# Decode attention over a cache: the last head's keys and softmax ahead of the preceding head's products with v

## The chip, the cores and the metric

The kernel runs on one core of one Trainium2 chip. The metric is device time in microseconds for one execution. The engines named below are PE (matrix products, with its own row PEld for weight loads), DVE and ACT (element-wise work, reductions, exponentials), POOL (one power per norm) and SP, which issues nearly all loads. All float data is 32 bits wide.

## The reference

Two layers, each an attention block and an MLP block, for one new token of width 640, with the same weights and the same cache in both layers:

```
x = x + attention(layernorm(x), k_cache, v_cache, wq, wo)
x = x + mlp(layernorm(x), w1, w2)
x = x + attention(layernorm(x), k_cache, v_cache, wq, wo)
x = x + mlp(layernorm(x), w1, w2)

attention(x): q = (x @ wq) in 32 heads of 128
              p = softmax(q . k * 128**-0.5) over 8192 cached positions
              o = p . v ;  return o (32*128 wide) @ wo
mlp(x):       return max(x @ w1, 0) @ w2          # hidden width 1728
```

The keys of one head are 8192 x 128 floats, 4 MB, and its values are another 4 MB; 32 heads make 268 MB, read once per layer apart from what is kept on the chip.

## The kernel before

**Head by head.** A head's keys come transposed, in four runs of four blocks. `scores` multiplies them by the head's query, which `spread` puts into one column of a 32-column operand, so that 16 rows of one 128 x 512 tile hold all 8192 scores (L366). `exponentials` takes the maximum of each row (L378) and the exponentials with their row sums (L385). `turn` brings the exponentials into columns (L393, L401). `rows_weighed` makes the weights by which the 16 rows, each with its own maximum, are put together (L406 to L416); it is a generator, and its steps are set between other work. `values` multiplies the turned exponentials by v (L427), and `output` copies the sums (L444, L445), multiplies them by the row weights on PE (L453) and leaves the head's 128 outputs in a column of `o_cols` (L460). For the last head of a layer `output` copies in two parts (L447, L449), so that the first copy does not wait for the last piece of v.

**The ring.** Keys and values go into one buffer, `ring`, of 3496 columns of eight floats: three halves of a head (1024 columns each) and 424 more. `todo` is the list of all loads in order. `pump` takes the next load from its head as soon as `place` finds a free stretch, and issues it on SP's queue (L133). It is called from `release`, that is, each time a piece has been used for the last time. One load waits behind another: SP issues them in order. Most heads are two loads of 4 MB, keys and values; the heads near the layers' ends are cut into smaller ones (`UNITS`). The last head of a layer has its keys in two loads of 2 MB and its values in four (2 MB, 1 MB, 768 KB, 256 KB); the head before it has, of its values, two of 2 MB.

**The turn between the layers.** Layer 0 goes through heads 0 to 31, layer 1 through heads 31 to 0. When layer 0 ends, the ring holds all of head 31 and the last of head 30's keys and its values. These stay and are used again by layer 1, so no load into the ring can begin until layer 1 has gone through a piece of head 31. The first four loads of head 30's keys go, for layer 1, into four weight buffers that have become free (`load_beside`, L147).

**The order on the engines.** The schedule is written out by hand: each engine does its instructions in the order of the program text. Work that is not a head's own (projections of earlier heads' outputs by `wo`, queries of the next four heads, products of weights that shorten the layer's end) stands in two lists, `chores` and `slow`; `side_work` does one PE step and one DVE step of them, and is called between the pieces of keys and of values. `due(h)` puts entries on the lists when head `h` begins. Two chores belong to the layer's end. `first_of_last` projects the first two heads of the last group of four. `before_last` projects the third (L332), adds the residual (L642), centres the row (`centred`, L245 to L259), in layer 0 begins layer 1's first query (L655), and makes five steps of `hidden` (L582): the MLP's first product for everything but the last head's share, which `mlp` adds when the last head's outputs are there. After the last head `mlp` finishes the layer; in layer 0 it also makes the query of head 31 for layer 1.

**Buffers that order work.** `p` is one buffer: a head's exponentials and the copy that `output` makes of a head's sums (`oc`) share it. `pT`, the turned exponentials, is one buffer, too. `h_t` holds a head's small columns. The score tiles `ps` are two banks.

**At the end of a layer**, before the change, the order on PE is: scores of the next-to-last head (30 in layer 0, 1 in layer 1), its `turn` and weights, its products with v, its `output`; then the last head's scores, with the steps of `before_last` between their pieces; its `turn` and weights; its products, with the rest of `before_last` after the second piece; its `output`; `mlp`.

Of the kernel before, what the change touches and what calls it, by code (L numbers as in the profile page):

```python
# [10 lines left out]
F32 = mybir.dt.float32  # L11
# [4 lines left out]
P = 128  # L16
D = 640
H = 32
# [5 lines left out]
HG = 4  # L24
# [16 lines left out]
UNITS = {h: WHOLE for h in range(H)}  # L41
# [38 lines left out]
def decode_kernel(ctx: ExitStack, tc: tile.TileContext, x, kv, wq, wo, w1, w2, out):  # L80
# [3 lines left out]
    work = ctx.enter_context(tc.tile_pool(name="work", bufs=1))  # L84
# [268 lines left out]
    def spread_column(q):  # L353
        nc.vector.tensor_copy(
# [3 lines left out]
    def spread(h):  # L358
        spread_column(qT[h // HG][:, h % HG : h % HG + 1])
# [79 lines left out]
    def output(hd, col):  # L439

        oc = work.tile([P, 5, DH], F32, name="p")
        pt = ps_m.tile([P, 512], F32, name="pm")
        if hd.out is hd.out_3:
            nc.vector.tensor_copy(oc[:, :2], hd.out[:, :2])  # L444
            nc.scalar.copy(oc[:, 2:4], hd.out[:, 2:])  # L445
        else:
            nc.vector.tensor_copy(oc[:, :3], hd.out[:, :3])  # L447
            yield
            nc.vector.tensor_copy(oc[:, 3], hd.out_3[:, 3])  # L449
            in_wait(384)  # L450
        n = 1 if hd.out is hd.out_3 else 64
        for r in range(4):
            nc.tensor.matmul(  # L453
                pt[:, :n],
                oc[:, r],
                hd.w[:, r : r + 1].to_broadcast([P, n]),
                start=(r == 0),
                stop=(r == 3),
            )
        nc.vector.tensor_copy(col, pt[:, :1])  # L460
# [130 lines left out]
    def attention_and_mlp(L, xr, s, before=None):  # L591
# [77 lines left out]
        def due(h):  # L669

            where = heads.index(h)
            k, j = divmod(where, HG)
            if j == 0:
                o_cols[k] = work.tile([P, HG], F32, name="o_cols", bufs=2)
            if where and j == 0:
                chores.append([run_out(k - 1), "pe"])
            if j == 2 and k + 1 < NG:
                slow.append([queries_of(k + 1), "pe"])
            if where == H - 2:
                chores.append([first_of_last(), "pe"])  # L680
            if where == H - 1:
                chores.append([before_last(), "pe"])
            if L == 0 and where == 4:
                nc.scalar.dma_start(w1_t, w1)
            if L == 0 and where == 7:
                nc.scalar.dma_start(w2_t, w2)
            if L == 0 and where == 9:
                n = NB * DH * (HG - 1)
                nc.scalar.dma_start(wqc.rearrange("p c d -> p (c d)"), wq[P * (NG - 1) :, n:])
            if L == 0 and where == MIX_AT[0][-1]:  # L690
                slow.append([centred_weights(), "pe"])
            if where == WC_AT[L]:
                nc.scalar.dma_start(mix[:, :D], wo[last // HG][:, last % HG])
            if where == WC_AT[L] + 1:
                slow.append([mixing(), "dve"])
            if where in MIX_AT[L]:
                slow.append([mixing_quarter(MIX_AT[L].index(where)), "pe"])
            if L == 0 and where == MIX_AT[L][-1] + 1:
                slow.append([leading_of_output(), "pe"])
            if where in LEAD_AT[L]:  # L700
                slow.append([leading(LEAD_AT[L].index(where)), "pe"])

        def side_work():
            work_off("pe")
            work_off("dve")
# [3 lines left out]
        def begun(where):  # L709

            nonlocal r
            h = heads[where]
            due(h)
            hd = Head(h)
            pieces = list(pieces_of(L, h, "k"))
            for a, (piece, at) in enumerate(pieces):
                scores(hd, piece, at, a == 0, a == len(pieces) - 1)
                if L and where == 0:
                    r = next(before)
                elif a < len(pieces) - 1:  # L720
                    side_work()
                if h == last and a == 1:
                    side_work()
            return hd

        hd = None
        for where, h in enumerate(heads):
            hd = hd or begun(where)
            if L and where == 0:
                exponentials(hd, r[0])  # L730
                xr, xc = next(before)
                load_wq(groups[1], nc.scalar)
            else:
                exponentials(hd)
            side_work()
            if h == last:
                side_work()
# [5 lines left out]
            hd.out = outs[count[0] % 2]  # L743
            count[0] += 1
            hd.out_3 = outs[count[0] % 2] if h == last else hd.out
            if h == last:
                o = work.tile([P, 1], F32, name="c_ol")
                rest = output(hd, o)
            pieces = list(pieces_of(L, h, "v"))
            for a, (piece, at) in enumerate(pieces):  # L750
                values(hd, piece, at, a == 0, a == len(pieces) - 1)
                if a == 0:
                    at_once(weighing)
                    if h != last:
                        spread(heads[where + 1])
                if a < len(pieces) - 1 and (h != last or a == 1):
                    side_work()
                if h == last and a == len(pieces) - 2:
                    next(rest)
            if h == last:  # L760
                at_once(rest)
            else:
                k, j = divmod(where, HG)

                ahead = begun(where + 1) if L and where < 2 else None
                at_once(output(hd, o_cols[k][:, j : j + 1]))
                hd = ahead
        assert not chores and not slow

        return mlp(L, o, last, *mlp_in)  # L770
# [236 lines left out]
```

## Time and profile before

| | us |
|---|---|
| runs of before (median of 3) | 1367.77 |
| runs of before, lowest and highest | 1365.71, 1371.56 |
| profiled execution, span from first to last instruction | 1368.2 |
| PE busy, whole span | 1006.9 |
| DVE busy, ACT busy | 182.4, 113.3 |

The profiled execution has no time of its own beside its span; the span lies within the runs. Mean granted clock of PE is 0.807. A line of the timeline gives the start in us from the first instruction, the busy time, the engine, the line of the kernel, the operation, what is written and read, its shape and count, and in brackets how long the engine was idle ahead of it and what ended that. On PE one product of float32 data appears as two instructions, so "x16" is eight products. A row that groups several instructions gives their busy time together. "DMA ring<-in_kv" is the landing of a load into the ring. `SPq L133` is the issue of such a load.

### The profile page before, as it was taken

How to read it: one execution, taken by the hardware profiler on the slowest of the kernel's cores; microseconds unless marked ns; L12 is line 12 of the kernel's file. 1: busy time of each engine (PE TensorE's matmuls, PEld its weight loads, DVE VectorE, ACT ScalarE, POOL GpSimd, SP SyncE). 2: the span in 40 equal slices, each digit the busy share in tenths (PEclk: the TensorE clock that was granted, in tenths of full speed). 3: DMA queues.
4: the chain of work that ended last, by engine and by line, in shares of the span. 5: the costliest groups of instructions: out<-in, count | busy, mean ns of one | idle time of the engine just before them, and what ended most of it. 6: DMA issues, size and time to landing. Idle time of an engine off the chain costs nothing.

```text
span 1368.2 us, 16729 instructions
## 1 busy us (share of the span) xinstructions
PE 1006.9 (74%) x7546; PEld 416.1 (30%) x7546; DVE 182.4 (13%) x696; ACT 113.3 (8%) x305; POOL 2.9 (0%) x10
## 2 busy tenths in 40 slices
PE   6564756777787878788798776667777687677668
PEld 2221212323333334343254322222223222222224
DVE  1010100111101101011122101110111111111112
ACT  0000000100111101011001000000001000000000
POOL 0000000000000000000000000000000000000000
PEclk8786777888878878888798778788878787788787
DMA  9999999999999999999979999999999999999994
GB/s 394 431 432 428 430 435 426 431 429 434 427 433 428 428 432 429 433 427 421 424 299 409 431 433 428 429 433 427 434 427 432 430 430 431 432 429 433 428 425 173
DMA packets 29023, 572.70 MB, mean 419 GB/s; under 512 B 3220, under 2 KB 3352, under 8 KB 5656
## 3 DMA queue, kind: packets, MB, share of 16 engines
q1 hardware_dynamic: 24200, 525.27, 89.8%
q10 hardware_dynamic: 4752, 46.37, 8.1%
q8 instruction: 59, 0.97, 0.3%
q14 instruction: 12, 0.10, 0.0%
HBM read 571.62 MB, written 0.00 MB: 418 GB/s over the span
## 4 chain that ended last, share of the span: by engine, by line
DMA 62%; PE 33%; DVE 2%; ACT 1%; issue 1%; SPq 0%; POOLq 0%; POOL 0%; ACTq 0%; DVEq 0%
DMA ring<-in_kv 61%; PE outs L427 12%; PE ps L366 11%; PE pt L393 2%; PE px L506 2%; ACT p L385 1%; DVE h_t L378 1%; DMA wqc<-in_wq 1%; PE px L312 1%; PE pm L413 1%; PE acc L582 1%; PE px L559 1%; PE acc L332 1%; PE pm L453 1%; PE px L551 0%
## 5 line engine op out<-in xcount | busy, mean ns | idle before, releaser
L366 PE MATMUL ps<-ring,spread_q 128*32 128x512 f32 (+2 forms) x2064 | 321.3, 735 | 178.4 <-DMA ring<-in_kv 178.4
L427 PE MATMUL outs<-ring,pT 128*4 128x512 f32 (+2 forms) x2128 | 325.7, 762 | 51.2 <-DMA ring<-in_kv 50.8
L366 PEld LDWEIGHTS ps<-ring,spread_q 128*32 128x32 f32 x2064 | 62.3, 127 | 291.7 <-DMA ring<-in_kv 188.6
L427 PEld LDWEIGHTS outs<-ring,pT 128*4 128x4 f32 x2128 | 57.8, 101 | 253.6 <-issue 192.1
L378 DVE TENSOR_REDUCE h_t<-ps 128x1 f32<-128x512 f32 x64 | 44.2, 691 | 471.4 <-PE ps L366 471.3
L453 PE MATMUL pm<-h_t,p 128*128 128x1 f32 (+1 forms) x512 | 69.9, 258 | 33.4 <-DVE p L444 33.1
L453 PEld LDWEIGHTS pm<-h_t,p 128*128 128x128 f32 x512 | 64.6, 194 | 94.9 <-DVE p L444 92.8
L385 ACT ACTIVATE p<-ps,h_t 128x512 f32<-128x512 f32 x63 | 43.3, 687 | 575.0 <-DVE h_t L378 547.5
L393 PE MATMUL pt<-row_of,p 128*128 128x16 f32 x512 | 69.9, 269 | 22.3 <-ACT p L385 22.2
L393 PEld LDWEIGHTS pt<-row_of,p 128*128 128x128 f32 x512 | 63.8, 196 | 34.2 <-ACT p L385 34.1
L444 DVE COPY p<-outs 128x256 f32<-128x256 f32 x62 | 26.3, 425 | 346.4 <-PE outs L427 346.4
L406 PE MATMUL pm<-ident,h_t 128*128 128x128 f32 x128 | 31.7, 330 | 40.2 <-DVE h_t L378 40.2
L445 ACT COPY p<-outs 128x256 f32<-128x256 f32 x62 | 23.1, 372 | 456.7 <-DVE p L444 456.7
L406 PEld LDWEIGHTS pm<-ident,h_t 128*128 128x128 f32 x128 | 19.4, 191 | 91.0 <-DVE h_t L378 88.4
L506 PE MATMUL px<-w_t,wct 128*128 128x448 f32 (+1 forms) x80 | 45.6, 656 | 0.0
L413 PE MATMUL pm<-h_t 128*128 128x1 f32 x128 | 27.4, 283 | 24.5 <-DVE h_t L410 24.5
L312 PEld LDWEIGHTS px<-wq_t,ln_xc 128*32 128x32 f32 x630 | 27.5, 155 | 17.7 <-issue 15.1
L312 PE MATMUL px<-wq_t,ln_xc 128*32 128x128 f32 x630 | 31.5, 367 | 1.6 <-DMA wq_t<-in_wq 1.6
L413 PEld LDWEIGHTS pm<-h_t 128*128 128x128 f32 x128 | 21.9, 214 | 30.8 <-DVE h_t L410 30.8
L332 PE MATMUL acc<-wo_t,o_cols 128*32 128x160 f32 x496 | 29.5, 395 | 0.0
L332 PEld LDWEIGHTS acc<-wo_t,o_cols 128*32 128x32 f32 x496 | 20.8, 145 | 18.9 <-issue 14.5
L506 PEld LDWEIGHTS px<-w_t,wct 128*128 128x128 f32 x80 | 13.5, 211 | 37.5 <-issue 36.0
(151 smaller groups left out, 350.8 us busy)
## 6 DMA issues: line engine op xcount, KB each, us to landing
ring<-in_kv SPq DMA_DIRECT2D x104, 4096.0 KB, 25.4
ring<-in_kv SPq DMA_DIRECT2D x27, 2048.0 KB, 24.0
ring<-in_kv SPq DMA_DIRECT2D x19, 1024.0 KB, 20.3
wo_t<-in_wo ACTq DMA_DIRECT2D x14, 1280.0 KB, 17.4
wq_t<-in_wq ACTq DMA_DIRECT2D x13, 1280.0 KB, 17.4
w_t<-in_w ACTq DMA_DIRECT2D x1, 4480.0 KB, 25.0
w_t<-in_w ACTq DMA_DIRECT2D x1, 4320.0 KB, 24.6
ring<-in_kv SPq DMA_DIRECT2D x3, 768.0 KB, 27.9
```

Of the source, the lines that this page charges most:

```text
L312: nc.tensor.matmul(pq[32 * j : 32 * j + 32, :DH], xc[:, c : c + 1].to_broadcast([P, 32]), weights_of(g, c, j), start=(c == 0), stop=(c == ...
L332: nc.tensor.matmul(acc[32 * g : 32 * g + 32, :DR], col.to_broadcast([col.shape[0], 32]), wt[:, g * DR : (g + 1) * DR], start=first, stop=last,
L366: nc.tensor.matmul(hd.ps[32 * g : 32 * g + 32, c : c + n], spread_q[:, 3 - r : 35 - r], tile_of[:, at + g * n : at + (g + 1) * n], start=f ...
L378: nc.vector.tensor_reduce(hd.nm, hd.ps, AX.X, ALU.max, negate=True)
L385: nc.scalar.activation(hd.p, hd.ps, AF.Exp, bias=hd.nm, scale=scale, accum_out=hd.l)
L393: nc.tensor.matmul(pt[:, 16 * b : 16 * b + 16], hd.p[:, b * P : (b + 1) * P], row_of.rearrange("p g r -> p (g r)"), start=True, stop=True,)
L406: nc.tensor.matmul(pt[:, :P], hd.nm.to_broadcast([P, P]), ident, start=True, stop=True)
L413: nc.tensor.matmul(pt[:, :1], hd.l.to_broadcast([P, P]), hd.wi, start=True, stop=True)
L427: nc.tensor.matmul((hd.out if r0 < 3 else hd.out_3)[32 * g : 32 * g + 4, r0:r1].rearrange("p r d -> p (r d)"), hd.pT[:, 4 * i : 4 * i + 4] ...
L444: nc.vector.tensor_copy(oc[:, :2], hd.out[:, :2])
L453: nc.tensor.matmul(pt[:, :n], oc[:, r], hd.w[:, r : r + 1].to_broadcast([P, n]), start=(r == 0), stop=(r == 3),)
L506: nc.tensor.matmul(pt[:, :n], wct[:, c], w1_t[:, c, f : f + n], start=(c == 0), stop=(c == NB - 1),)
```

## The change

At the end of both layers the list of loads is put in another order: the last two heads' keys first, then the last two heads' values. In layer 0 that is keys of 30, keys of 31, values of 30, values of 31; in layer 1 keys of 1, keys of 0, values of 1, values of 0. The work follows that order. When the next-to-last head has its exponentials turned and its weights complete, the last head's query is spread, its scores, exponentials and weights are made, and only then come the next-to-last head's products with v. Then the last head's exponentials are turned, ahead of the next-to-last head's `output`, because they share `p`. `before_last` is put on the list after that `output`; four of its seven PE steps are done at once, the other three between the pieces of the last head's products. So that two heads can be under way, `h_t` becomes two buffers of 8 columns in place of one of 16, and the columns `wi` and `rl` share the places of `low` and `nm`.

```diff
-    todo = [(0, u) for u in order]
-    todo += [(1, (h, i)) for h in range(H)[::-1] for i in range(len(UNITS[h])) if (h, i) not in kept]
+    todo = []
+    for L, heads in enumerate((range(H), range(H)[::-1])):
+        units = [(h, i) for h in heads for i in range(len(UNITS[h]))]
+        end = [u for u in units if u[0] in heads[-2:]]
+        end = [u for kind in "kv" for u in end if UNITS[u[0]][u[1]][0] == kind]
+        units = [u for u in units if u not in end] + end
+        todo += [(L, u) for u in units if not L or u not in kept]
...
-            t = work.tile([P, 16], F32, name="h_t")
+            t = work.tile([P, 8], F32, name="h_t", bufs=2)
             self.w = t[:, :4]
-            self.nm, self.l, self.low, self.wr, self.wi, self.rl = (
-                t[:, i : i + 1] for i in range(4, 10)
-            )
+            self.nm, self.l, self.low, self.wr = (t[:, i : i + 1] for i in range(4, 8))
+            self.wi, self.rl = self.low, self.nm
...
-        for where, h in enumerate(heads):
-            hd = hd or begun(where)
+        for where, h in enumerate(heads[:-1]):
+            if hd is None:
+                due(h)
+                hd = begun(where)
...
+            ahead = None
+            if where == H - 2:
+                at_once(weighing)
+                spread(last)
+                ahead = begun(where + 1)
+                exponentials(ahead)
+                side_work()
+                at_once(rows_weighed(ahead))
             pieces = list(pieces_of(L, h, "v"))
             for a, (piece, at) in enumerate(pieces):
                 values(hd, piece, at, a == 0, a == len(pieces) - 1)
...
+            if L and where < 2:
+                due(heads[where + 1])
+                ahead = begun(where + 1)
+            elif where == H - 2:
+                turn(ahead)
+            k, j = divmod(where, HG)
+            at_once(output(hd, o_cols[k][:, j : j + 1]))
+            hd = ahead
+
+        assert not chores and not slow
+        due(last)
...
+        rest = output(hd, o)
+        for _ in range(4):
+            side_work()
+        pieces = list(pieces_of(L, last, "v"))
+        for a, (piece, at) in enumerate(pieces):
+            values(hd, piece, at, a == 0, a == len(pieces) - 1)
+            if a < len(pieces) - 2:
+                side_work()
+            if a == len(pieces) - 2:
+                next(rest)
+        at_once(rest)
```

More of the change, by code (lines that the diff above doesn't have):

```diff
@@ L712, in begun @@
             h = heads[where]
-            due(h)
             hd = Head(h)
@@ L721, in begun @@
                     side_work()
-                if h == last and a == 1:
-                    side_work()
             return hd
         hd = None
-        for where, h in enumerate(heads):
-            hd = hd or begun(where)
+        for where, h in enumerate(heads[:-1]):
+            if hd is None:
+                due(h)
+                hd = begun(where)
             if L and where == 0:
@@ L735, in attention_and_mlp @@
             side_work()
-            if h == last:
-                side_work()
             weighing = rows_weighed(hd)
@@ L742, in attention_and_mlp @@
             next(weighing)
-            hd.out = outs[count[0] % 2]
+            hd.out = hd.out_3 = outs[count[0] % 2]
             count[0] += 1
[L745 to L748, printed above, removed]
+            ahead = None
[6 more added lines that the diff above has]
+                at_once(rows_weighed(ahead))
             pieces = list(pieces_of(L, h, "v"))
@@ L751, in attention_and_mlp @@
                 values(hd, piece, at, a == 0, a == len(pieces) - 1)
-                if a == 0:
+                if a == 0 and where < H - 2:
                     at_once(weighing)
-                    if h != last:
-                        spread(heads[where + 1])
-                if a < len(pieces) - 1 and (h != last or a == 1):
+                    spread(heads[where + 1])
+                if a < len(pieces) - 1:
                     side_work()
[L758 to L767, printed above, removed]
+            if L and where < 2:
[8 more added lines that the diff above has]
+        due(last)
+        hd.out, hd.out_3 = outs[count[0] % 2], outs[(count[0] + 1) % 2]
+        count[0] += 1
+        o = work.tile([P, 1], F32, name="c_ol")
+        rest = output(hd, o)
[9 more added lines that the diff above has]
+        at_once(rest)
         assert not chores and not slow
```

## The prediction

> **What bounds the kernel now.** I read the page first: the load rate in 40 slices and the chain that ended last, by engine.
>
> ```profile
> span 1368.2 us, 16729 instructions
> ...
> GB/s 394 431 432 428 430 435 426 431 429 434 427 433 428 428 432 429 433 427 421 424 299 409 431 433 428 429 433 427 434 427 432 430 430 431 432 429 433 428 425 173
> ...
> DMA 62%; PE 33%; DVE 2%; ACT 1%; issue 1%; SPq 0%; POOLq 0%; POOL 0%; ACTq 0%; DVEq 0%
> ```
>
> The loads run at about 430 GB/s in every slice but three: the first, slice 21 (299) and the last (173). Nothing in the change alters the bytes, so it can move time only at the two ends of a layer, where the loads stop. The windows of those two places come next (columns: length, busy time of PE, its weight loads, DVE, ACT, POOL, granted clock, DMA share, GB/s).
>
> ```profile
> 697.00:703.00 6.00, 5.62 (x72) 3.41 (x68) 1.73 (x6) 1.07 (x3) 0.00 (x0) 1.00 0.65 260
> 703.00:709.00 6.00, 5.68 (x71) 3.28 (x64) 1.58 (x6) 0.39 (x3) 0.00 (x0) 1.00 0.08 29
> ...
> 1318.00:1331.00 13.00, 8.90 (x84) 3.97 (x83) 1.97 (x8) 1.23 (x4) 0.00 (x0) 1.00 1.01 430
> ...
> 1336.00:1339.00 3.00, 3.00 (x18) 1.61 (x21) 0.16 (x1) 0.00 (x0) 0.00 (x0) 0.50 1.03 437
> 1339.00:1342.00 3.00, 3.00 (x27) 1.22 (x19) 0.33 (x2) 0.00 (x0) 0.00 (x0) 0.50 0.98 412
> ...
> 1352.00:1358.00 6.00, 5.75 (x82) 3.27 (x78) 0.94 (x4) 0.00 (x0) 0.00 (x0) 1.00 0.01 3
> ```
>
> So at both ends PE works alone while the loads stand. Now the timeline there: what PE waited for at the end of layer 0 (head 31's second half of keys), when that layer's last product piece is done (L447 copies it), and when layer 1's loads can begin. Then, for layer 1, the copy after its last products.
>
> ```profile
> 694.47 0.37 PEld L366 LDWEIGHTS ps<-ring,spread_q 128*32 128x32 f32 x8 [0.38 <-DMA ring<-in_kv]
> ...
> 705.06 0.56 DVE L447 COPY p<-outs 128x384 f32<-128x384 f32 x1 [3.63 <-PE outs L427]
> ...
> 714.37 131.80 SPq L133 DMA_DIRECT2D ring<-in_kv  x22
> ...
> 1331.76 2.96 PE L427 MATMUL outs<-ring,pT 128*4 128x512 f32 x16 [2.52 <-DMA ring<-in_kv]
> ...
> 1355.66 0.56 DVE L447 COPY p<-outs 128x384 f32<-128x384 f32 x1 [3.64 <-PE outs L427]
> ```
>
> The reader should see that the first load of layer 1 is issued at 714.37, about 9 us after head 31's products: the ring is full of kept data until layer 1 has used some of it. Whatever delays PE at the end of layer 0 delays all of layer 1's loads by as much.
>
> Two more loads must be dated: the issue rows of SP, each with its size and time to landing from the DMA view of that instant.
>
> ```profile
> 674.87 0.33 SPq L133 DMA_DIRECT2D ring<-in_kv  x1
> ...
> ring<-in_kv SPq DMA_DIRECT2D x1, 256.0 KB, 29.4
> ...
> 1317.26 0.33 SPq L133 DMA_DIRECT2D ring<-in_kv  x1
> ...
> ring<-in_kv SPq DMA_DIRECT2D x1, 2048.0 KB, 24.2
> ...
> 1323.46 0.42 SPq L133 DMA_DIRECT2D ring<-in_kv  x1
> ...
> ring<-in_kv SPq DMA_DIRECT2D x1, 256.0 KB, 28.2
> ```
>
> The last value piece of layer 0 lands at 674.87 + 29.4 = 704.3, of layer 1 at 1323.46 + 28.2 = 1351.7. Head 0's second half of keys lands at 1317.26 + 24.2 = 1341.5.
>
> **The change, part by part.**
>
> *Queue order.* At each layer's end the last head's keys (two loads of 2 MB) go ahead of the preceding head's values (two of 2 MB). I replayed the placement rule of `place` on both orders: load for load the slots have the same sizes and the same releases free them, so issue times stay. What moves is who sits in which place. The preceding head's second value half takes the place that the last head's second key half had: head 30's lands at 694.4 (the wait in row 694.47), head 1's at 1341.5. Before, it landed 2 x 4.9 = 9.8 us earlier (4 MB at the 430 GB/s of the row): at 1331.7 by row 1331.76 for head 1, and at about 684.6 for head 30. The final value loads land when they did.
>
> *What hangs on that half.* In program order after it: its products, `turn` of the last head, the copy of the outputs and the four matmuls of `output` (L444, L453), the projection of head 30's (head 1's) column, the residual (L642), the centring, five `hidden` steps, and, between these, all products of the last head. `turn` stands ahead of the copy because both use the one buffer named p, so it is new on this path. Only after the last `hidden` can the MLP's first product take the last head's share. What leaves the path: the last head's scores, its exponentials and its row weights. Prices at full clock, from this trace:
>
> ```profile
> 664.90 1.90 PE L427 MATMUL outs<-ring,pT 128*4 128x512 f32 x16 [2.17 <-DMA ring<-in_kv]
> ...
> 657.80 1.06 PE L393 MATMUL pt<-row_of,p 128*128 128x16 f32 x8 [0.38 <-ACT p L385]
> ...
> 658.90 0.22 DVE L401 COPY pT<-pt 128x64 f32<-128x64 f32 x1 [1.16 <-PE pt L393]
> ...
> 666.87 0.42 DVE L444 COPY p<-outs 128x256 f32<-128x256 f32 x1 [6.63 <-PE outs L427]
> ...
> 667.35 1.06 PE L453 MATMUL pm<-h_t,p 128*128 128x1 f32 x8 [0.55 <-DVE p L444]
> ...
> 690.12 0.16 DVE L460 COPY o_cols<-pm 128x1 f32<-128x1 f32 x1 [1.16 <-PE pm L453]
> ...
> 690.89 0.45 PE L332 MATMUL acc<-wo_t,o_cols 128*32 128x160 f32 x8
> ...
> 691.41 0.33 DVE L642 SCALAR_TENSOR_TENSOR xr<-acc,xr 128x160 f32<-128x160 f32 x1 [1.14 <-PE acc L332]
> ...
> 693.52 0.51 PE L655 MATMUL px<-wqc,ln_xc 128*32 128x128 f32 x9 [0.51 <-DVE ln_xc L259]
> ...
> 702.55 0.92 PE L582 MATMUL acc<-w_t,ln_xc 128*32 128x448 f32 x8
> ...
> 700.83 1.91 PE L427 MATMUL outs<-ring,pT 128*4 128x384 f32 x32
> ...
> 703.26 1.94 PE L427 MATMUL outs<-ring,pT 128*4 128x384 f32 x32
> ```
>
> Products 1.90; `turn` to the end of its copy 1.32 (657.80 to 659.12); copy to L453 0.48; L453 to its result 1.11 (1.06 and a hand-over); the column and the projection 0.2 + 0.45; L642 to the first matmul on the centred column 2.11 (691.41 to 693.52) and 0.07 before it: 7.64 us. Then five hidden steps 4.60 and the last head's products 3.85, of which the last narrow piece (0.15) is beside the copy: 8.3. In layer 0 L655 adds 0.51. Together 15.9 us in layer 1, 16.4 in layer 0, with the last value pieces (704.3, 1351.7) landed before PE reaches them.
>
> - Layer 0: 694.45 + 16.4 = 710.9 against 705.06, **+5.8 us**. The rest up to 714.37 is the same code, so layer 1's loads and all of layer 1 start that much later.
> - Layer 1: 1341.5 + 15.9 = 1357.4 against 1355.66, **+1.8 us**.
>
> *The clock.* The layer-1 tail of before ran at clock 0.50 through its first part. The same kinds of work there:
>
> ```profile
> 679.64 1.89 PE L393 MATMUL pt<-row_of,p 128*128 128x16 f32 x8
> ...
> 1335.24 1.86 PE L453 MATMUL pm<-h_t,p 128*128 128x1 f32 x8 [0.53 <-DVE p L444]
> ...
> 1338.74 0.76 PE L332 MATMUL acc<-wo_t,o_cols 128*32 128x160 f32 x8
> ...
> 1339.57 0.33 DVE L642 SCALAR_TENSOR_TENSOR xr<-acc,xr 128x160 f32<-128x160 f32 x1 [2.27 <-PE acc L332]
> ...
> 1343.07 1.71 PE L582 MATMUL acc<-w_t,ln_xc 128*32 128x448 f32 x8 [0.60 <-DVE ln_xc L259]
> ```
>
> At that clock the chain up to the first hidden step is 2.96 (row 1331.76) + 2.14 + 0.48 + 1.90 + 0.96 + 0.07 + about 2.7 (between the 2.11 of layer 0 and the 3.50 from 1339.57 to 1343.07, in which key scores stood too) = 11.2 instead of 7.64: +3.6. In layer 1 of the changed kernel PE waits for one 2 MB load after the other (4.9 us each) ahead of 1341.5, with half a score or product set (about 1.9) and some row weights for each. In before an idle stretch of 2.52 (row 1331.76) was enough for half clock, so I take half clock up to the first hidden step there: +5.4. In layer 0 the same gap stands ahead of 694.4, but head 31's scores, dense work, come late (after 681.5, where the `turn` of row 679.64 ends); half clock is as likely as not, so I take the middle of 5.8 and 9.4: +7.6. Ends: both full, 5.8 + 1.8 = +7.6; both half and one hidden-and-products stretch more at half (1.7 each, two steps at 0.8 more), 11.1 + 7.1 = +18.2.
>
> By the Trainium skill, "TensorE: Matmul & The Clock Gate", Part 1, the clock comes back after about 3.4 us of sustained work. By that rule the tails would be cold for little more than the value half, and the sum would be about 1378 instead of 1381. This trace does not agree: in 1336 to 1342 PE was busy 6.00 of 6.00 us and the clock stayed 0.50, so I keep the longer cold stretch.
>
> *Parts at nothing.* `h_t` is 8 columns in two buffers for 16 in one; the two shared columns (`wi` on `low`, `rl` on `nm`) are written after the readers that those same steps already wait for. The side work that stood in the last head's key loop is now four steps ahead of its products: counted above. The ring slots that layer 1 frees first hold the same kinds of data. The 320 KB load behind L655 falls into the standing time of the loads and holds nothing up.
>
> *Sum:* 1368.2 + 7.6 + 5.4 = 1381.2; this execution lies 0.4 over the median of the runs, so 1381.
>
> **The rivals.**
>
> 1. *The clock is full in both tails, or returns early.* For: layer 0's tail ran at 1.00 (row 697.00). Full: 1375.8, chance 0.10. If it returns once the value half is through, each end costs the 1.06 of the products (2.96 for 1.90) and some 0.2 of `turn` over full clock: 7.6 + 2.5, 1378, chance 0.12; against it the two rows at 0.50. The page named above speaks for the second. Both are still slower.
> 2. *Layer 0's delay is absorbed.* Layer 1 begins on data kept in the ring, so a late start of its loads might be made up. For: PE waits for loads through most of the layer. Against: those loads are the bound and wait for PE's first release (714.37), with 29 GB/s moved just before; a gap there is not won back. Then only layer 1's end counts: 1370 to 1373.6. Chance 0.08.
> 3. *Faster: the value half is not late.* If the queue had slack, so that swapping two loads cost v less than its transfer time, the softmax would leave the path for nothing: in layer 0 the 3.4 us from this row to the first products (700.83).
>
> ```profile
> 697.45 0.69 DVE L378 TENSOR_REDUCE h_t<-ps 128x1 f32<-128x512 f32 x1 [3.98 <-PE ps L366]
> ```
>
> It decides from a delay under about 4 us per end. At best the ends come to the last landings: 0.5 us in layer 0, 1355.66 - 1351.9 = 3.7 in layer 1, 1364. Against: the DMA share is 0.98 to 1.03 while these very loads move. Chance 0.05.
>
> **How the numbers follow.** Forecast 1381, chance 0.60; rivals 0.22, 0.08, 0.05; another 0.05 for more than 1387. The range, 1373 to 1387, takes both ends of the clock (1375.8, 1386.4) and the upper edge of the absorbed case. About 0.5% (6.8 us) is what a measurement here can tell from no change; the three runs of before span 5.9 us. Slower by more: 0.60 + 0.05 + most of rival 1 (0.19) = 0.84. Within: rival 2 and the rest of rival 1, 0.11. Faster: 0.05.
>
> **What would show it.** Head 30's (head 1's) second value half is waited for at about 694 (1341 + the delay), at L427. After it the order L393, L444, L453, L332, L642, then hidden steps between products, with no L366 or L378 among them. Layer 1's first load is issued at 720 to 725 instead of 714.37. The 299 of slice 21 falls. From the last landing to the end of layer 1's products pass some 9 us where 4 passed. If the v half lands as early as before, the theory is wrong at its root; if it lands late and the L447 copies come no later, the chain is mis-sized.

## The result, and the profile after

The changed kernel takes 1383.76 us (median of 5 runs, 1379.10 to 1384.36) against 1367.77 for the kernel before: 1.0104 times as long, with a 95% interval of 1.0092 to 1.0115. By the medians that is 16.0 us more; by the ratio, which goes by all the runs, it is about 14 us (12.6 to 15.7). Ratios and intervals here leave out executions in a slow state, which concerns two of the twelve runs with the residual first (1386.84 and 2757.63 us). The profiled execution has a span of 1377.3 us and is the quickest of the five (1379.10); the others have spans of 1379.2 to 1382.6 and lower mean clocks (0.800, 0.801, 0.801 and 0.808 against 0.810). A second profile of the changed kernel, below, shows one of those.

The page of the changed kernel: span, load rate in 40 slices, and the chain that ended last.

```profile
span 1377.3 us, 16677 instructions
...
GB/s 394 436 427 432 428 431 430 428 428 434 429 432 431 428 427 432 433 424 424 425 228 414 432 432 428 430 432 429 432 432 429 429 428 431 433 431 429 431 425 128
...
DMA 65%; PE 31%; DVE 2%; ACT 1%; issue 1%; SPq 0%; POOLq 0%; POOL 0%; ACTq 0%; DVEq 0%
```

Slice 21 has fallen from 299 to 228 GB/s and the last from 173 to 128; the rest is as it was. So the time was lost where the prediction looked for it, at the two ends. The timeline at the end of layer 0 of the changed kernel (lines of the changed file: L431 is `values`, L397 `turn`, L457 the products of `output`, L337 the projection, L646 the residual, L659 and L586 the first matmuls on the centred column, L451 the first copy after the last products):

```profile
694.32 0.11 PEld L431 LDWEIGHTS outs<-ring,pT 128*4 128x4 f32 x8 [1.72 <-DMA ring<-in_kv]
...
696.30 1.06 PE L397 MATMUL pt<-row_of,p 128*128 128x16 f32 x8
...
697.55 0.41 DVE L448 COPY p<-outs 128x256 f32<-128x256 f32 x1
...
698.02 1.09 PE L457 MATMUL pm<-h_t,p 128*128 128x1 f32 x8 [0.65 <-DVE p L448]
...
699.90 0.33 DVE L646 SCALAR_TENSOR_TENSOR xr<-acc,xr 128x160 f32<-128x160 f32 x1 [0.60 <-PE acc L337]
...
701.67 0.85 PE L659 MATMUL px<-wqc,ln_xc 128*32 128x128 f32 x9 [0.51 <-DVE ln_xc L264]
...
707.50 0.56 PE L586 MATMUL acc<-w_t,ln_xc 128*32 128x416 f32 x3
...
709.11 0.56 PE L586 MATMUL acc<-w_t,ln_xc 128*32 128x416 f32 x3
...
711.03 0.56 DVE L451 COPY p<-outs 128x384 f32<-128x384 f32 x1 [9.42 <-PE outs L431]
...
720.26 6.56 SPq L138 DMA_DIRECT2D ring<-in_kv  x4
```

Head 30's second value half is waited for at 694.32, in the place of the queue where head 31's second key half stood. From there PE needs 16.7 us to the copy at 711.03; before, it needed 10.6 from that moment (694.47 to 705.06). The first load of layer 1 follows 9.2 us later as before, now at 720.26 in place of 714.37. The end of layer 1:

```profile
1347.25 1.90 PE L431 MATMUL outs<-ring,pT 128*4 128x512 f32 x16 [0.71 <-DMA ring<-in_kv]
...
1354.75 3.20 PE L586 MATMUL acc<-w_t,ln_xc 128*32 128x448 f32 x16 [0.60 <-DVE ln_xc L264]
...
1364.80 0.56 DVE L451 COPY p<-outs 128x384 f32<-128x384 f32 x1 [10.19 <-PE outs L431]
```

Head 1's value half comes at 1347.25. That is 5.75 us after 1341.5, which is layer 0's delay (5.89 at the first load) and little else. From there the copy is 17.55 us away; before, it was 14.16 (1341.5 to 1355.66), so this chain adds 3.39. Together that is 5.75 + 3.39 = 9.14 us, and 1368.2 + 9.1 = 1377.3.

### The profile page after: what moved, and what is told of

The parts are those of the page before. It is cut to its first block, busy times and chain, and to the rows that moved or that the text cites. A ratio compares the mean times of both kernels' runs of the same rounds, so it can differ in the third digit from the quotient of the medians.

```text
span 1377.3 us, 16677 instructions
## 1 busy us (share of the span) xinstructions
PE 1006.2 (73%) x7546; PEld 413.0 (30%) x7546; DVE 182.5 (13%) x696; ACT 113.2 (8%) x305; POOL 2.9 (0%) x10
## 4 chain that ended last, share of the span: by engine, by line
DMA 65%; PE 31%; DVE 2%; ACT 1%; issue 1%; SPq 0%; POOLq 0%; POOL 0%; ACTq 0%; DVEq 0%
DMA ring<-in_kv 65%; PE outs L431 10%; PE ps L370 10%; PE px L510 2%; PE pt L397 2%; ACT p L389 1%; PE px L317 1%; PE acc L586 1%; DVE h_t L382 1%; PE acc L337 1%; PE pm L417 1%; PE px L563 1%; PE pm L457 1%; PE px L543 0%; DVE pT L405 0%
## 5 line engine op out<-in xcount | busy, mean ns | idle before, releaser
L431 PE MATMUL outs<-ring,pT 128*4 128x512 f32 (+2 forms) x2128 | 329.4, 764 | 49.8 <-DMA ring<-in_kv 49.5
L431 PEld LDWEIGHTS outs<-ring,pT 128*4 128x4 f32 x2128 | 60.4, 101 | 257.1 <-issue 190.1
L457 PE MATMUL pm<-h_t,p 128*128 128x1 f32 (+1 forms) x512 | 68.3, 255 | 33.6 <-DVE p L448 33.3
L457 PEld LDWEIGHTS pm<-h_t,p 128*128 128x128 f32 x512 | 62.9, 190 | 92.0 <-DVE p L448 89.8
L397 PE MATMUL pt<-row_of,p 128*128 128x16 f32 x512 | 69.6, 268 | 22.8 <-ACT p L389 22.6
L397 PEld LDWEIGHTS pt<-row_of,p 128*128 128x128 f32 x512 | 63.3, 195 | 36.3 <-ACT p L389 34.4
L337 PE MATMUL acc<-wo_t,o_cols 128*32 128x160 f32 x496 | 27.4, 374 | 0.5 <-DVE o_cols L464 0.5
L405 DVE COPY pT<-pt 128x64 f32<-128x64 f32 x64 | 14.4, 225 | 84.4 <-PE pt L397 84.4
## 6 DMA issues: line engine op xcount, KB each, us to landing
ring<-in_kv SPq DMA_DIRECT2D x19, 1024.0 KB, 20.2
```

Source lines behind the costliest of these rows:

```text
L337: nc.tensor.matmul(acc[32 * g : 32 * g + 32, :DR], col.to_broadcast([col.shape[0], 32]), wt[:, g * DR : (g + 1) * DR], start=first, stop=last,
L397: nc.tensor.matmul(pt[:, 16 * b : 16 * b + 16], hd.p[:, b * P : (b + 1) * P], row_of.rearrange("p g r -> p (g r)"), start=True, stop=True,)
L431: nc.tensor.matmul((hd.out if r0 < 3 else hd.out_3)[32 * g : 32 * g + 4, r0:r1].rearrange("p r d -> p (r d)"), hd.pT[:, 4 * i : 4 * i + 4] ...
L457: nc.tensor.matmul(pt[:, :n], oc[:, r], hd.w[:, r : r + 1].to_broadcast([P, n]), start=(r == 0), stop=(r == 3),)
```

## The experiments

Each run was also timed beside the kernel before on the same chip; ratios are to that. The word chain stands below for the stretch from the landing of the second load of the last pair that changes places (head 31's or head 0's second key half before, head 30's or head 1's second value half after) to the first copy behind the last products. The value half is the second half of the next-to-last head's values.

### The change in one layer only

```diff
-        end = [u for u in units if u[0] in heads[-2:]]
+        end = [u for u in units if u[0] in heads[-2:] and L in (0,)]   # (1,) in the second run
...
-        def begun(where):
+        if L in WORK:            # the changed loop; WORK is (0,) or (1,)
...
+        else:                    # the loop of before
```

> The change (order of loads and order of work) in layer 0 only; layer 1's end as before. Theory (at each end the chain on PE starts from the same landing as before, but is longer: 16.4 us from the preceding head's second value half instead of 10.6 us from the last head's second key half, and a later end of layer 0 delays every load of layer 1): +5.8 to +9.5 us over before, with the first load of layer 1 issued 5.8 to 9.5 us later. Rival (layer 0's delay is absorbed in layer 1): within 1.5 us of before.

> The change in layer 1 only. Theory: +1.8 us (clock full in the tail) to +7 us (half until into the hidden steps), and together with the run of layer 0 alone it adds up to the whole change (+16 us). Rival (layer 0's delay is absorbed, all of the loss is here): the whole +14 to +16 us.

Layer 0 alone: 1377.78 us against 1369.86, ratio 1.0056 (1.0035 to 1.0077), +7.9. Layer 1 alone: 1375.06 against the same, 1.0039 (1.0026 to 1.0052), +5.2. Together +13.1. The timeline with layer 0 alone changed:

```profile
694.50 2.62 PE L432 MATMUL outs<-ring,pT 128*4 128x512 f32 x16 [2.79 <-DMA ring<-in_kv]
...
714.71 0.56 DVE L452 COPY p<-outs 128x384 f32<-128x384 f32 x1 [10.01 <-PE outs L432]
...
723.94 6.56 SPq L139 DMA_DIRECT2D ring<-in_kv  x4
...
1342.00 1.90 PE L432 MATMUL outs<-ring,pT 128*4 128x512 f32 x16 [0.92 <-DMA ring<-in_kv]
...
1363.23 0.56 DVE L452 COPY p<-outs 128x384 f32<-128x384 f32 x1 [3.64 <-PE outs L432]
```

The windows of its two chains (columns as before):

```profile
694.50:714.70 20.20, 18.33 (x166) 11.57 (x166) 1.43 (x7) 0.37 (x1) 0.00 (x0) 0.66 0.34 134
1351.70:1363.20 11.50, 10.68 (x132) 5.61 (x132) 1.99 (x8) 1.07 (x3) 0.00 (x0) 1.00 0.51 207
```

Layer 0's chain took 20.2 us here, at a clock of 0.66, and every load of layer 1 came later with it: head 1's value half is used at 1342.00 in place of 1331.76. Nothing of the delay was absorbed. Layer 1's tail, unchanged, took 11.5 us at clock 1.00 (its start, 1351.8, is worked out from issue and time to landing), not the 14.2 of the profile before. In the run with layer 1 alone changed the value half is used at 1341.58, as forecast for that place, and the copy comes 17.5 us later:

```profile
1341.58 1.90 PE L432 MATMUL outs<-ring,pT 128*4 128x512 f32 x16 [0.77 <-DMA ring<-in_kv]
...
1359.07 0.56 DVE L452 COPY p<-outs 128x384 f32<-128x384 f32 x1 [9.95 <-PE outs L432]
```

### The loads alone, the work alone

```diff
 # loads alone: todo as in the change, the loop over heads as before
 # work alone: the changed loop over heads, and
-        end = [u for u in units if u[0] in heads[-2:]]
+        end = [u for u in units if u[0] in heads[-2:] and L in ()]
```

> Only the order of the loads is changed, in both layers; the work keeps its order of before (next-to-last head's products, then the last head's scores and exponentials, then its products). Theory (the load order costs, because the value half lands 9.8 us later; the new work order wins back a part of it): 18.5 us of chain after that landing in place of 10.6, +8 in layer 0 and +4 to +10 in layer 1: 1380 to 1386, not faster than the whole change by more than 2 us. Rival (the new order of work costs, by turn ahead of output and by a cold PE): within 3 us of before.

> Only the order of the work is changed; the loads keep their order, so the last head's keys are waited for ahead of the next-to-last head's products, whose data lies ready. Theory: from the last head's second key half (same landing as ever) PE has its scores 1.9, weights 2.5, the next-to-last head's products 3.6, then the rest of the chain 14.5: 22.5 us in place of 10.6, +12 in layer 0 and +8 to +12 in layer 1: 1387 to 1392, the slowest of all. Rival (the new work order is cheap and only its own turn and the shared buffer cost, 1.3 us an end): up to 1371.

Both of these kernels have the change's two buffers of `h_t`. Loads alone: 1384.02 us against 1369.86, 1.0106 (1.0090 to 1.0123), as expected. Work alone: 1399.09, 1.0212 (1.0174 to 1.0250); 1387 to 1392 was expected, so this cost was put too low. The timelines of the ends of layer 0, first with the loads alone, then with the work alone:

```profile
694.18 1.90 PE L431 MATMUL outs<-ring,pT 128*4 128x512 f32 x16 [1.43 <-DMA ring<-in_kv]
...
712.67 0.56 DVE L451 COPY p<-outs 128x384 f32<-128x384 f32 x1 [3.63 <-PE outs L431]
```

```profile
694.55 3.65 PE L370 MATMUL ps<-ring,spread_q 128*32 128x512 f32 x16 [1.16 <-DMA ring<-in_kv]
...
724.24 0.56 DVE L451 COPY p<-outs 128x384 f32<-128x384 f32 x1 [10.76 <-PE outs L431]
```

In both, and in the whole change, the wait ends between 694.1 and 694.6: what is second in that pair lands there, whatever it is. What follows differs: 18.5 us with the loads alone, as reckoned, at a clock of 1.00, and 29.7 with the work alone (22.5 was reckoned; the clock granted there was 0.64). The swap of the loads by itself costs as much as the whole change. Beside the loads alone (18.5 us in layer 0, 19.8 in layer 1 at clock 0.90), the chains of the changed kernel's profile are 1.8 and 2.3 us shorter, but the times (1384.0 and, further down, 1382.2) do not tell the two apart.

### Half of the delay

```diff
-        end = [u for kind in "kv" for u in end if UNITS[u[0]][u[1]][0] == kind]
+        end = sorted(end, key=lambda u: (u[0] == heads[-1] and u[1] > 0,
+                                         u[0] != heads[-1] and UNITS[u[0]][u[1]][0] == "v"))
 # only the last head's first key half goes ahead of the values; the loop over heads as before
```

> Work in the order of before; of the last head's keys only the first half (2 MB) is loaded ahead of the next-to-last head's values, so that their second half lands 4.9 us later than before in place of 9.8. Theory (the time follows the landing of the value half): from the value half at about 689.5 the 18.5 us chain that the run with only the loads changed showed ends at 708.0 against 705.1, +3 us in layer 0 and 0 to +3 in layer 1, so +3 to +6 us over before where the whole delay cost +14. Rival (any swap of the loads costs by itself, as by their places in the ring): +10 us or more.

> The kernel with half of the swap once more, for a second profile: its first profile (1372.8) had both tails at clock 1.00, its other runs took 1378 to 1381. Theory (the difference is the clock in the tails): with a time near 1380 the chains from the value half to the copy after the last products are longer than the 18.5 us of the first profile by 7 us in sum, and the granted clock there is under 1.00. Rival (something else between the tails is slower): the same 18.5 and 18.2 us, and the extra time in the stretch between the first load of layer 1 and its last loads.

This kernel, too, has the change's two buffers of `h_t`. Four runs took 1372.82 to 1380.75, median 1379.25 against 1367.83, which is +11.4. The ratio is 1.0072 (1.0052 to 1.0093), or 7 to 13 us. A later single run took 1376.67, beside 1370.50 for the kernel before. So by the times the theory's +3 to +6 us is missed, and the rival's +10 or more is nearer. Only the profiled run, the quickest of the four (1372.82), is where the theory wanted it. Its timeline:

```profile
689.43 1.90 PE L431 MATMUL outs<-ring,pT 128*4 128x512 f32 x16 [1.66 <-DMA ring<-in_kv]
...
707.92 0.56 DVE L451 COPY p<-outs 128x384 f32<-128x384 f32 x1 [3.64 <-PE outs L431]
...
1340.11 1.90 PE L431 MATMUL outs<-ring,pT 128*4 128x512 f32 x16 [1.30 <-DMA ring<-in_kv]
...
1358.25 0.56 DVE L451 COPY p<-outs 128x384 f32<-128x384 f32 x1 [3.64 <-PE outs L431]
```

In layer 0 the value half comes 4.75 us sooner than with the loads alone (694.18 to 689.43) and the copy 4.75 us sooner (712.67 to 707.92): the same chain of 18.5 us, moved. In this execution the time follows the landing. The second profile has a longer first tail; the windows from the value half to the copy, first profile, then second:

```profile
689.40:707.90 18.50, 17.03 (x202) 9.64 (x202) 3.03 (x12) 1.44 (x4) 0.00 (x0) 1.00 0.64 263
```

```profile
689.80:710.00 20.20, 18.67 (x202) 9.72 (x202) 3.03 (x12) 1.44 (x4) 0.00 (x0) 0.91 0.58 238
```

It was not near 1380 and so does not show what made those runs longer. Of the 3.8 us between the two spans (1371.0 and 1374.8) the first chain at clock 0.91 accounts for 1.7, and 1.5 lie behind the last copy, where the clock of the second profile fell to 0.50 (1366 to 1368). In neither profile do the ring's places cost anything between the ends: from layer 1's first load to the landing of head 0's second key half, which here has the place that the value half has in the full swap, 627.7 and 628.0 us pass, where the profiles without any swap have 626.5 to 628.6. Why three other runs took 1378 to 1381 stays open.

### The changed kernel again, and with PE kept busy

```diff
+                if h == last and a == 2:            # ahead of the last head's second key half
+                    in_wait(384)
...
+                in_wait(256)                        # behind its scores
...
+                if where == H - 2 and a == 2:       # ahead of the value half
+                    in_wait(512)
...
                 turn(ahead)
+                in_wait(192, "px")
...
             projected(acc, runs[-1][2:], o_cols[NG - 1][:, 2:], False, True)
+            in_wait(128, "px")
```

`in_wait` multiplies a part of `w1` by the identity into a bank that nobody reads.

> The changed kernel once more, beside the runs below on the same chip. Theory (what its executions differ by, 1379 to 1384, is how much of the two tails is at half clock): +12 to +16 us over before, and in this profile each tail's excess over before (layer 0: 5.8 at full clock, layer 1: 1.8) goes with the clock granted from the value half's landing to the copy after the last products.

> The changed kernel with idle matmuls put on PE where it waits in the two tails (ahead of the last head's second key half, behind its scores, ahead of the value half, behind turn and behind the projection). Theory (clock term): both tails come near full clock, 5.8 + 1.8 over before and up to 1 us for the idle matmuls, so 1375 to 1379, that is 4 to 8 us faster than the changed kernel. Rival (the half clock is no part of the loss, the chain is just longer than reckoned): no faster than the changed kernel.

The changed kernel again: 1382.19 us against 1368.39, 1.0105 (1.0088 to 1.0122). With the idle matmuls: 1379.99, 1.0085 (1.0070 to 1.0100): 2.2 us less, not 4 to 8. The intervals overlap, but all four runs (1379.85 to 1380.37) lie under the four beside them (1381.30 to 1385.32). The windows of the chains, for the first profile of the changed kernel (three stretches in layer 0, three in layer 1), then for the second:

```profile
694.30:699.10 4.80, 4.15 (x36) 2.28 (x32) 0.56 (x2) 0.37 (x1) 0.00 (x0) 0.96 0.86 360
699.10:701.70 2.60, 1.38 (x25) 0.94 (x25) 0.88 (x5) 0.00 (x0) 0.00 (x0) 0.96 0.52 214
701.70:711.00 9.30, 9.30 (x114) 6.11 (x114) 0.00 (x0) 0.00 (x0) 0.00 (x0) 0.83 0.19 60
1347.20:1351.90 4.70, 3.98 (x32) 2.29 (x32) 0.56 (x2) 0.37 (x1) 0.00 (x0) 1.00 0.90 373
1351.90:1354.70 2.80, 1.57 (x20) 1.13 (x20) 0.87 (x5) 0.00 (x0) 0.00 (x0) 0.78 0.52 216
1354.70:1364.80 10.10, 10.05 (x104) 5.33 (x104) 0.00 (x0) 0.00 (x0) 0.00 (x0) 0.72 0.06 23
```

```profile
694.40:712.30 17.90, 16.03 (x166) 9.95 (x166) 1.43 (x7) 0.37 (x1) 0.00 (x0) 0.81 0.40 159
1349.50:1368.20 18.70, 16.68 (x157) 8.70 (x157) 1.44 (x8) 0.37 (x1) 0.00 (x0) 0.74 0.30 124
```

The second profile's chains are 17.9 and 18.7 us, 2.3 more in sum than the first's, at clocks of 0.81 and 0.74; its span is 3.4 us longer, with most of the rest between the two ends (627.9 us there, 626.9 in the first profile). In layer 0 the order goes with the clock: 16.7 us at 0.89 (the first three rows weighted), 17.9 at 0.81, 20.2 at 0.66 in the run with layer 0 alone changed. Where in the chain the half clock stands shows in four windows of the second profile, layer 1:

```profile
1349.00:1351.00 2.00, 1.42 (x8) 0.26 (x12) 0.00 (x0) 0.00 (x0) 0.00 (x0) 0.50 1.02 424
...
1353.00:1355.00 2.00, 1.35 (x12) 1.26 (x12) 0.55 (x2) 0.37 (x1) 0.00 (x0) 1.00 0.57 237
...
1359.00:1361.00 2.00, 1.97 (x12) 0.73 (x16) 0.00 (x0) 0.00 (x0) 0.00 (x0) 0.50 0.00 0
...
1363.00:1365.00 2.00, 2.00 (x40) 1.39 (x36) 0.00 (x0) 0.00 (x0) 0.00 (x0) 1.00 0.00 0
```

The value half runs at half clock, `turn` and `output` at full clock, the first hidden steps at half clock again. In the other three chains of the two profiles the clock is full from the value half, or from its first microsecond, on, and falls about 6 to 7 us behind its landing, around the centring; it is back 3.4 to 6.9 us later. With the idle matmuls the clock fell all the same, in the middle of layer 0's chain:

```profile
694.40:697.50 3.10, 3.10 (x23) 0.88 (x22) 0.00 (x0) 0.00 (x0) 0.00 (x0) 1.00 0.96 400
697.50:700.90 3.40, 2.92 (x25) 2.09 (x24) 1.04 (x5) 0.37 (x1) 0.00 (x0) 1.00 0.59 245
700.90:704.30 3.40, 2.77 (x29) 2.40 (x33) 0.38 (x2) 0.00 (x0) 0.00 (x0) 0.50 0.31 122
```

PE was busy 2.92 of 3.40 us and was then at half clock for 3.4 us. In that stretch stand `turn` and `output`, whose matmuls stream 16 columns and one. Idle matmuls stand on the chain itself, too. In layer 0 they gained nothing: from the landing at 694.4 to the copy 18.6 us pass at clock 0.82. In layer 1 the chain took 16.2 us at 0.89, where the two profiles without them have 17.6 and 18.7 at 0.81 and 0.74. So within the changed kernel the longer chains go with the lower clocks, and what the clock term is worth stays open.

### Without `turn` on the chain

```diff
-    def turn(hd):
+    def turn(hd, room=None):
...
-        hd.pT = work.tile([P, 16 * NBL], F32, name="pT")
+        hd.pT = room if room is not None else work.tile([P, 16 * NBL], F32, name="pT")
...
                 at_once(rows_weighed(ahead))
+                turn(ahead, work.tile([P, DR], F32, name="q_row")[:, : 16 * NBL])
...
-            elif where == H - 2:
-                turn(ahead)
```

> The changed kernel with the last head's turn put ahead of the next-to-last head's products, into the wait for the value half (its result goes to the free q_row buffer). Theory: turn and its copy leave the chain after the landing, 1.3 us at full and 2.1 us at half clock per end: 2.6 to 4.2 us faster than the changed kernel, still 8 us or more slower than before. Rival (the new order of work, with turn ahead of output, is the main cost): most of the loss goes.

1381.26 us (1376.83 to 1383.28), 1.0099 (1.0081 to 1.0117) to before: 0.9 us under the changed kernel beside it, with intervals that overlap, so the 2.6 to 4.2 us that were expected are not shown in the times. In the profile, which is of the quickest run, the chain of layer 0 is shorter by what was reckoned:

```profile
694.35 1.90 PE L431 MATMUL outs<-ring,pT 128*4 128x512 f32 x16 [0.32 <-DMA ring<-in_kv]
...
709.89 0.56 DVE L451 COPY p<-outs 128x384 f32<-128x384 f32 x1 [9.52 <-PE outs L431]
```

15.5 us in place of 16.7 in the first profile of the changed kernel, both at clock 0.89. The rival is out: most of the loss stays.

### Can the kernel before be improved at these ends?

```diff
 # first run, on the kernel before: PE kept busy at layer 1's end
+                if L and h == last and a == 2:
+                    in_wait(384, "px")
...
+                if L and where == H - 2 and a == 2:
+                    in_wait(512)
+                    in_wait(512)
 # second run, on the kernel before: the residual ahead of the last head's scores
             hd = Head(h)
+            for _ in range(2 if h == last else 0):
+                side_work()
...
-                if h == last and a == 1:
-                    side_work()
...
-                if a < len(pieces) - 1 and (h != last or a == 1):
+                if a < len(pieces) - 1 and h != last:
```

> The kernel before with idle matmuls on PE at layer 1's end only (ahead of head 1's second value half and ahead of head 0's second key half). Theory: layer 1's tail of before, at half clock from 1332.5 to 1346, comes to the same 10.6 us after the last key half that layer 0 shows at full clock, so the copy after the last products comes at about 1352.2 in place of 1355.7: 2 to 3.5 us faster than before. Rival (that tail is bound by the landings): within 0.5 us of before.

> The kernel before, loads and heads in its order, with only the last head's side work moved: the projection of the next-to-last head's column, the residual and the centring stand ahead of the last head's first scores (in the wait for its keys), and the last two hidden steps stand in its softmax in place of behind its second value piece. Theory (before, the residual's chain waits behind scores that wait for the last head's first key half, 15 us from that half to the copy after the last products): the chain from the second key half falls from 10.6 to 11.9 us to about 10 in layer 0, from 11.5 to 14.2 to 10.5 to 12 in layer 1, with 9.9 and 10.2 as the floor set by the last value landing: 1 to 4 us faster than before. Rival (the tails of before are at the landings already): within 1 us.

> The kernel before once more, for a second profile. Theory: span = a fixed part (about 1343.6 us) + the two chains from the last head's second key half to the copy after the last products, 10.4 to 11.9 us in layer 0 and 11.5 to 14.2 in layer 1, depending on the clock granted there.

Neither helps: 1369.44 us against 1368.39, 1.0009 (1.0000 to 1.0018), with PE kept busy, and 1368.3 (median of ten runs) against 1367.83, 1.0004 (0.9991 to 1.0016), with the residual first. With PE kept busy the clock still fell to 0.50 (1339 to 1341), and layer 1's tail took 12.2 us, not 10.6. With the residual first the profile has 10.7 and 10.3 us for the two tails, as hoped, but the times are no shorter. The second profile of the kernel before (a single run of 1367.2 us, span 1365.1) shows how little there is to gain. Its layer 1 tail:

```profile
1342.17 1.07 PE L366 MATMUL ps<-ring,spread_q 128*32 128x512 f32 x8 [0.34 <-DMA ring<-in_kv]
...
1352.15 0.22 PEld L427 LDWEIGHTS outs<-ring,pT 128*4 128x4 f32 x8 [0.42 <-DMA ring<-in_kv]
...
1352.53 0.56 DVE L447 COPY p<-outs 128x384 f32<-128x384 f32 x1 [3.64 <-PE outs L427]
```

PE waits for the last value load and is done 0.4 us behind it: this execution is at the landings already, with a chain of 10.4 us. Its tail in layer 0 took 11.8 us, and the sum that was expected, 1343.6 + 11.8 + 10.4 = 1365.8, is near its span. The 14.2 us of the first profile went with half clock from 1334 to 1346. What was to be gained at this end is there in some executions only, and it does not show in the median. No kernel tried is faster than the one before.

## Why the prediction was right

*Where the time moves.* Right: the two ends, and nothing between. The stretch from the first load of layer 1 to the use of the value half (or of what stands in its place) was about 627 us before (714.37 to 1341.5) and is 627.0 now (720.26 to 1347.25). Worked out from the issues and times to landing of SP's loads, for the load in the second place of the pair, it is 626.5 to 628.6 us in all fourteen profiles, whatever was changed at the ends.

*The queue order.* Right: 694.45 and 1341.5 were forecast as landings, and 694.32 and 1347.25 (1341.4 without layer 0's delay) were seen; the run with layer 1 alone changed has 1341.58.

*The chain.* Right in its parts and their order, and somewhat long. Up to the first matmul on the centred column 7.64 us was reckoned for full clock and 7.35 measured (694.32 to 701.67, clock 0.96). The five hidden steps with the four pieces of the last products were put at 8.3 us by adding busy times of single groups. Where the clock is full, one hidden step and one product piece take 1.61 us together (707.50 to 709.11) and not 1.88 (0.92 + 0.96), which makes 1.1 us over four such pairs. So the chain at full clock was reckoned about 1.4 us too long.

*The clock.* Half clock was there, as forecast, but mostly not where it was put. It was expected from the value half up to the first hidden step. In three of the four chains of the changed kernel's two profiles the clock was full there, and half from around the centring into the hidden steps. The prediction took the wait ahead of the value half to be an idle one. In the first profile's layer 1 the products of the first half ran at half clock and filled most of that wait: PE was idle for 0.71 us ahead of 1347.25. In the second profile's layer 1 it was idle for 2.27 us, and there the value half ran at half clock. That the size came out all the same is luck.

*Layer 0:* +7.6 forecast, as the middle of two clocks; the run with layer 0 alone gave +7.9. That fit is partly luck, too: in its profile layer 0's copy comes 9.65 us later than before (705.06 to 714.71), and layer 1's tail is 2.7 us shorter (11.5 for 14.2). In the changed kernel's two profiles layer 0's chain is 16.7 and 17.9 us long, where 16.4 was reckoned for full clock and 20.0 for half.

*Layer 1:* +5.4 forecast, +5.2 in the run with layer 1 alone. The size is right by two errors that cancel. The comparison was with the 14.2 us tail of one profile of before, partly at half clock; two other executions show 11.5 and 10.4. And 19.5 us was reckoned for the new chain, where the first profile has 17.6, the second 18.7 and the run with layer 1 alone 17.5.

*The sum.* 1381 forecast, 1383.76 measured, within 1373 to 1387. The part runs add to +13.1, as forecast. The change itself is +16.0 and, repeated, +13.8 by the medians; by the ratios it is +14.2 (12.6 to 15.7) and +14.4 (12.0 to 16.7). With the intervals of the part runs (+4.8 to +10.5 and +3.6 to +7.1) these do not contradict each other, and no gap between them is shown.

*The rivals.* The absorbed delay is out (layer 0 alone, +7.9, with all of layer 1's loads later). The value half that is not late is out (694.32, and the swap of loads alone, +14.2). Full clock in both tails was not seen in any profile of the changed kernel. The early return of the clock is a rival whose premise came and whose time did not. Once the value half was through, the clock was full in every chain of these two profiles, but it fell again within a few us: in the second profile the layer 1 chain is 18.7 us long at a mean clock of 0.74 between 0.50 and 1.00, which makes 9.7 us at half clock (0.26 / 0.5 of 18.7), with PE busy 16.68 of 18.70. Against its 1378 us stand medians of 1383.76 and 1382.19. The Trainium skill, "TensorE: Matmul & The Clock Gate", Part 1, has the clock return after some 3.4 us of sustained work. In the first profile's layer 1 chain PE worked without a gap from 1354.75 on and the clock was back at about 1360.2, that is after some 5.4 us, so here it took longer, and the measurement decides.

## What to carry to other kernels

Here the loads on SP's queue landed in the order of their issue, and the second place of the pair landed at 694.1 to 694.8 us whichever load stood there; moving one load up moved another down by its whole transfer time (4.9 us for 2 MB). Ask of both what hangs on them. The keys' chain (scores, softmax, products) was 10.6 us long and hid the residual's chain beside it, and the values' chain in the same place was 16.7 us, since the projection, the residual, the centring and the hidden steps all wait for it. So of the data at the end of such a stream, let what has the longest chain behind it land first. A tail at a stage's end is best judged from several executions: layer 1's tail, with the same code, took 14.2 us with half clock from 1334 to 1346, 11.5 with half clock only just ahead of its start (0.50 from 1347.9 to 1349.9, start at 1351.8), and 10.4 at full clock.

## What was not expected of the hardware

The clock fell to 0.50 after a stretch in which PE was busy 2.92 of 3.40 us (697.50 to 700.90, with the idle matmuls), so a PE row that is busy for 86% of a stretch did not keep the clock there. Weight loads took 2.09 us of it, and its matmuls had one to 192 columns; what the clock goes by is not shown. And the landing at the end of layer 0, by issue and time to landing, came between 694.1 and 694.8 us in all fourteen profiles, whatever PE was doing, while the chains behind it differed by several us between executions of the same program.
